# A fused attention and channel-mix kernel: the whole plan of steps put in another order

## The chip, the cores and the metric

The kernel runs on one core of a Trainium2 chip. The metric is device time in microseconds. Before the change it is 189.6 us, the median of three runs (189.48 to 189.63). Inputs and output are float32; the kernel computes in bfloat16 with sums in float32.

## The reference

Eight batches of 576 tokens, eight heads of width 64. Each head's keys and values are first pooled into 32 memories, with a softmax of `phi` over the tokens; the queries then attend to the 32 memories. The result, 512 wide, goes through a channel mix.

```
a   = softmax(phi, over tokens)                  # [b, h, 576, 32]
k_m = a^T k ;  v_m = a^T v                       # [b, h, 32, 64]
x   = softmax(q k_m^T / 8, over memories) v_m    # [b, 576, 512]
x_prev = x shifted by one token (zeros first)
xk  = mu_k * x + (1 - mu_k) * x_prev ;  xr the same with mu_r
key = relu(xk @ w_k)            # 512 -> 1024
out = sigmoid(xr @ w_r) * ((key * key) @ w_v)
```

## The kernel before

**How the work is staged.** Batch 0 goes the plain way. Its pooled k and v are made (`ekv`, L312; `kg` and `vg` are the halves for two groups of heads, `z` sums the weights in L322 and takes the reciprocal `rz` in L326), k is scaled and turned (`norm_k` and `tr_k`: `h0`, `h1`, `tk`), q is turned on VectorE (`turn_q`, L381: `q0`, `q1`), scores (`s0`, `s1`, L395) and their exponentials (`es`) follow, then the denominators (`l`: sum and logarithm, `r`: exponential of its negative, `y`: the weighing). `mixed` (L355: `mk`, `mr`) forms the token-mixed x for keys and gates; `unload` (`uk`, `ur`) copies it from PSUM to `x0T`. Sixteen keys (`c0`, L599; `a` are 256 tokens, `b` are 320) are then matmuls of `x0T` with `wk`.

Batches 1 to 7 fold the pooled v into the weights instead: v is turned (`vt`, L463, with a copy to `vT`), `project` (L492: `G`) multiplies it with `wk` and `wr`, and `keep_g` (`E`) copies the product `G` from PSUM. The keys are then *pair keys* (`c1` to `c7`, L617 and L625): two matmuls for a first part, a copy `pa` to `pb`, and four matmuls that add the difference between neighbour tokens. The softmax sums are made on VectorE by two turns and a reduction (`fe`, `fs`, `fo`: L435, L441, L447), and `w` weighs (L458). Every key is read by a relu (`r`, or the second part of `c0`) and squared (`s`). The relus keep their results in five buffers named `rl`. Gates (`g`, `t`) are matmuls followed by a tanh; outputs (`o`, L760) are eight matmuls over the squares and `wv`, multiplied by the gate on VectorE (L771) and stored.

**What sets the order.** The text table `PLAN` is the whole schedule. Each word names one step, or one part of a step, and the words are issued one after the other. Each engine takes its own instructions in that order and waits where an operand is not ready. After `/` stands the engine for copies, relus and squares (`a` ScalarE, `d` VectorE); after `@` stand the PSUM banks (numbered 0 to 7) in which the step puts its results; a bank is written only when its last reader is done. `p:` words put a load in GpSimd's queue: an f32 array in HBM, written as bf16 but for `phi`. `b:NxM` words are N filler matmuls of M times 64 columns on zeros, whose results nobody reads. Ten fillers (`WARM`) stand before the plan in both versions.

GpSimd's queue issues loads in order. In the trace before, the ninth load is issued at 10.38 us, when the first has landed, and those after it one by one as earlier ones land.

Of the kernel before, what the change touches and what calls it, by code (L numbers as in the profile page):

```python
# [19 lines left out]
    "p:q:0b 0:c01/d 0:exp1 p:v:0h 0:c00/a 0:exp0 b:11x6@5 0:mub@0 0:mub 0:kg0@12 0:c10/d 0:c11/a b:2x8@5 0:kg1",  # L20
    "0:z@0 0:q0 0:z 0:h1/a p:v:0g 0:h0/a b:7x7@5 0:tk@3 0:tk 0:q1 b:2x6@5 0:s0@1204 0:s1@3567 0:es00 0:es10",
    "0:l00@1 0:l00 b:1x4@0 0:l10@2 0:l10 0:r00 0:y00 0:r10 0:y10 0:es01 0:es11 b:9x8@0 0:l11@4 0:l01@7 0:l01",
    "0:r01 0:vg1@65 0:vg0 0:y01 0:nk0 0:l11 0:nk1 0:r11 0:y11 b:5x7@0 0:mk1@7321 0:uk11/a p:wk:4-8 0:mu@4",
    "p:wk:2-4 0:uk10/d c0:3b@0 c0:4b@2 0:tb p:wk:0-2 c0:1b@1 c0:1b/d 0:nr1 c0:3b/a c0:3b/d p:phi:1 c0:0b@7 0:nr0",
    "c0:0b/d c0:2b@0 c0:2b/d c0:4b/a 1:exp c0:1b/a c0:4b/a c0:5b@5 0:mk0@6123 0:uk00/d c0:0b/d c0:5b/a c0:2b/a",
    "c0:6b@7 0:uk01/a c0:6b/a c0:5b/d 1:z@5 0:mr0@6021 0:ur01/a 0:mu c0:7b@3 0:ur00/a c0:3a@0 c0:0a@1 c0:0a/a",
    "p:q:1 0:mr1@2674 c0:7b/d c0:7b/d 1:z c0:2a@5 c0:6b/d 0:ur10/a c0:1a@1 c0:1a/a c0:2a/a c0:5a@2 1:q1 c0:0a/a",
    "c0:6a@7 c0:7a@1 c0:2a/a c0:6a/a c0:1a/a p:k:1 1:q0 c0:3a/d 1:k@53 p:wr:0-4 1:nk/d g:01@7 1:tk@3 p:wv:2-4",
    "1:tk c0:5a/a c0:5a/a c0:3a/a c0:4a@5 p:v:1 0:ur11/a c0:7a/a c0:7a/d c0:4a/a c0:4a/d 1:s@2063 1:es1 1:es0",
    "1:fe 1:fs g:02@4 g:03@6 g:01 g:03 o:02b@0 g:00@6 x:0/a c0:6a/d g:02 1:v@23 o:03b@5 1:fo 1:nv/a 1:vt@3 1:vm",  # L30
    "g:00 1:vt/d p:phi:2 o:00b@2 o:03b 2:exp o:00b 1:G00@64 1:Gs0@37 1:G01@51 1:Es00/a 1:E001/a o:02b o:01b@2",
    "1:w0 1:w1 1:Es01/a 1:d p:wv:0-2 o:00a@0 o:00a o:01a@7 p:v:2 o:01a o:01b 1:E000/a c1:0@6 1:E010/a 1:E011/a",
    "1:Gs1@05 1:Es11/a 1:G02@14 1:E021/a 1:E020/a 1:D0 1:Gs2@73 1:Es20/d c1:0/d@5 o:02a@2 o:02a 1:Es10/a c1:2@4",
    "o:03a@7 o:03a c1:2/a@0 1:Es21/a c1:0 1:D1 c1:7@2 p:q:2 2:q0 r:100/a p:k:2 c1:7/a@3 c1:2 c1:4@6 r:120/a 2:q1",
    "c1:4/a@1 c1:7 r:170/a c1:6@4 r:171/a c1:4 r:140/d r:101/a s:10/d c1:5@2 c1:6/a@3 r:141/a s:14/a c1:5/d@5",
    "1:D2 g:11@7 r:121/a s:17/d 2:z@6 2:z c1:6 r:160/a c1:5 2:kv@10 c1:3@4 r:161/a g:11/a@3 c1:1@6 r:150/d",
    "r:151/d 2:nk/d 2:nv/d g:11 2:vt@0 c1:1/d@5 s:12/a 2:tk@1 c1:3/a@2 2:vt/d c1:3 p:phi:3 t:110 p:phi:4 2:tk",
    "t:111 r:130/a s:16/d 2:vm r:131/a c1:1 r:110/d 2:s@1437 s:13/d g:e0@0 r:111/a s:11/d 2:Gs0@65 2:es1 2:es0",
    "g:e0 s:15/d 2:fe 2:Es01/a p:k:3 2:fs 2:fo 2:G00@17 x:1/d 2:Gs1@43 2:Es00/a 3:exp 2:w0 o:13@2 g:10@6 2:Es11/a",
    "3:z@5 2:E000/a 3:z o:12@0 o:13 o:12 p:q:3 p:v:3 g:10/a@1 2:Es10/a g:10 2:E001/a 3:q1 t:100 2:D0 t:101",  # L40
    "2:Gs2@75 2:Es20/a 2:w1 2:d 2:Es21/a 2:G02@24 3:kv@63 2:G01@10 3:nk/a 2:E011/a o:e0@7 o:e0 p:q:4 c2:0@0",
    "2:E010/a 2:D1 c2:0/d@1 3:nv/a 2:E021/a 4:exp c2:2@6 o:10@3 3:q0 c2:2/a@7 o:10 3:tk@4 c2:0 2:E020/a c2:4@2",
    "c2:2 r:200/a r:201/a c2:4/a@1 3:tk r:220/d 4:q0 3:s@4035 r:221/a 3:es1 3:es0 p:v:4 c2:3@6 c2:3/d@7 s:20/d",
# [809 lines left out]
```

## Time and profile before

| | |
|---|---|
| median of three runs | 189.6 us |
| the profiled execution: first to last instruction (span) | 187.8 us |
| its own whole time | not shown; the median is 1.8 us above the span |
| TensorE (PE) busy | 181.2 us, 96% |
| VectorE (DVE) busy | 153.9 us, 82% |
| ScalarE (ACT) busy | 151.9 us, 81% |
| GpSimd (POOL) busy | 30.2 us, 16% |
| granted TensorE clock | 1.00 throughout |

A matmul counts as busy from its start to its modelled end, and these overlap; so a busy TensorE is judged by the distance between starts. VectorE and ScalarE also start an instruction before the one ahead has quite ended. "Idle before" is time in which an engine had nothing running, with what ended it. `PEld` is the load of weights, which runs beside the matmuls.

### The profile page before, as it was taken

The numbers are of one execution on the slowest core, as the hardware profiler recorded it, in microseconds if no ns is written. First come the engines' busy times: TensorE is split into PE (matmuls) and PEld (weight loads), VectorE is DVE, ScalarE is ACT, GpSimd is POOL, SyncE is SP. The second block draws the span as 40 slices with busy tenths as digits, with TensorE's granted clock in tenths as the row PEclk, the third lists the DMA queues.
The fourth block names the chain that finished last, engine by engine and source line by source line (L and its number), as shares of the span: only waits on it lengthen the run. The fifth ranks groups of instructions, "written<-read, shape, count | busy, mean of one in ns | idle before, by whom it ended". The sixth has DMA issues, their size and how long they took to land.

```text
span 187.8 us, 6010 instructions
## 1 busy us (share of the span) xinstructions
PE 181.2 (96%) x2483; PEld 103.2 (55%) x2483; DVE 153.9 (82%) x328; ACT 151.9 (81%) x368; POOL 30.2 (16%) x46
## 2 busy tenths in 40 slices
PE   7979999999999999999999999999999999999992
PEld 2544566677644575556544655556545653465441
DVE  2334574899989999999999899999989999889441
ACT  2537889889999999999999889958999678775900
POOL 5943531060303040140032000000000010000000
PEclk9999999999999999999999999999999999999999
DMA  5999999999999999899989995114202224242054
GB/s 188 280 203 220 251 207 205 266 208 234 308 208 210 275 292 255 160 220 224 223 163 237 234 278 197 28 59 113 56 0 59 58 59 113 56 108 63 0 139 140
DMA packets 24923, 31.91 MB, mean 170 GB/s; under 512 B 1880, under 2 KB 19040, under 8 KB 24896
## 3 DMA queue, kind: packets, MB, share of 16 engines
q0 software_dynamic: 17936, 20.45, 59.0%
q1 hardware_dynamic: 5664, 9.00, 17.2%
q10 hardware_dynamic: 1296, 2.08, 3.3%
q8 instruction: 19, 0.31, 0.7%
q14 instruction: 8, 0.07, 0.1%
HBM read 38.28 MB, written 9.44 MB: 254 GB/s over the span
## 4 chain that ended last, share of the span: by engine, by line
PE 90%; DMA 4%; DVE 2%; issue 1%; ACT 1%; POOL 0%; POOLq 0%; DVEq 0%
PE pv L760 34%; PE pk L617 8%; PE pk L625 8%; PE pb L625 7%; PE gps L492 6%; PE pk L599 4%; DMA q<-in_q_dram 4%; PE pr L687 3%; PE pb L687 3%; PE pr L679 3%; PE kvps L312 3%; PE pr L709 2%; PE pr L666 2%; PE scps L395 2%; PE idle L259 1%
## 5 line engine op out<-in xcount | busy, mean ns | idle before, releaser
L760 PE MATMUL pv<-wv,sq 128*128 128x512 bf16 (+3 forms) x296 | 60.5, 350 | 0.0
L760 PEld LDWEIGHTS <-sq 128*128 128x128 bf16 x296 | 27.7, 98 | 24.9 <-issue 2.8
L498 ACT CAST G<-gps 128x512 bf16<-128x512 f32 x67 | 36.2, 629 | 1.2 <-PE gps L492 1.2
L771 DVE SCALAR_TENSOR_TENSOR o<-sg,pv 128x512 f32<-128x512 f32 (+3 forms) x41 | 24.9, 613 | 7.5 <-PE pv L760 5.1
L625 PEld LDWEIGHTS <-G 128*128 128x128 bf16 x224 | 21.4, 98 | 8.5 <-issue 0.7
L583 ACT ACTIVATE rl<-pk 128x288 bf16<-128x288 f32 (+2 forms) x49 | 20.0, 420 | 4.5 <-PE pk L625 3.9
L625 PE MATMUL pk<-diff,G 128*128 128x288 bf16 x112 | 22.9, 286 | 0.0
L625 PE MATMUL pb<-diff,G 128*128 128x288 bf16 x112 | 22.9, 286 | 0.0
L617 PE MATMUL pk<-atn,G 128*128 128x288 bf16 x112 | 20.8, 287 | 0.0
L621 ACT COPY pb<-pk 128x288 f32<-128x288 f32 x41 | 16.4, 410 | 5.1 <-PE pk L617 3.5
L591 DVE TENSOR_TENSOR sq<-rl 128x576 bf16<-128x576 bf16 (+2 forms) x46 | 18.3, 420 | 1.0 <-ACT rl L583 0.5
L583 ACT ACTIVATE rl<-pb 128x288 bf16<-128x288 f32 x40 | 16.2, 427 | 2.2 <-PE pb L625 1.8
L589 ACT ACTIVATE sq<-rl 128x576 bf16<-128x576 bf16 (+2 forms) x26 | 15.7, 624 | 0.5 <-DVE rl L585 0.4
L501 DVE TENSOR_TENSOR G<-G 128x1024 bf16<-128x1024 bf16 x21 | 14.3, 679 | 1.3 <-ACT G L498 1.3
L458 DVE TENSOR_TENSOR atn<-e,lz 128x576 bf16<-128x576 bf16 (+2 forms) x18 | 12.1, 683 | 3.5 <-ACT lz L430 3.5
L617 PEld LDWEIGHTS <-G 128*128 128x128 bf16 x112 | 10.2, 98 | 6.6 <-issue 1.5
L656 ACT ACTIVATE sg<-pr 128x512 f32<-128x512 f32 x22 | 13.0, 618 | 0.7 <-PE pr L687 0.6
L259 PE MATMUL idle<-zeros 128*128 128x512 bf16 (+3 forms) x47 | 12.2, 408 | 1.0 <-DVE zeros L187 1.0
L381 DVE STREAM_TRANSPOSE qT<-q 128x576 uint32<-128x576 uint32 (+2 forms) x16 | 12.1, 765 | 1.2 <-DMA q<-in_q_dram 1.2
L585 DVE TENSOR_SCALAR rl<-pk 128x288 bf16<-128x288 f32 (+2 forms) x23 | 10.1, 449 | 2.8 <-PE pk L599 2.6
L498 DVE CAST G<-gps 128x512 bf16<-128x512 f32 x17 | 11.3, 679 | 0.2 <-PE gps L492 0.2
L292 ACT ACTIVATE em<-ph 128x1152 bf16<-128x1152 f32 (+1 forms) x9 | 9.9, 1095 | 1.6 <-DMA ph<-in_phi_dram 1.6
(101 smaller groups left out, 283.7 us busy)
## 6 DMA issues: line engine op xcount, KB each, us to landing
out_dram<-o SPq DMA_DIRECT2D x46, 128.0 KB, 2.4
ph<-in_phi_dram POOLq DMA_DIRECT2D x7, 576.0 KB, 12.2
q<-in_q_dram POOLq DMA_DIRECT2D x7, 576.0 KB, 13.6
kv<-in_k_dram POOLq DMA_DIRECT2D x7, 576.0 KB, 14.2
kv<-in_v_dram POOLq DMA_DIRECT2D x7, 576.0 KB, 15.0
out_dram<-o SPq DMA_DIRECT2D x6, 256.0 KB, 6.5
out_dram<-o SPq DMA_DIRECT2D x20, 64.0 KB, 2.5
k0f<-in_k_dram ACTq DMA_DIRECT2D x2, 576.0 KB, 5.8
```

The source lines that it names most:

```text
L259: nc.tensor.matmul(ps.rearrange("p (a b) -> p a b", b=64), lhsT=zeros, rhs=zeros[:, :64].unsqueeze(1).to_broadcast([128, blocks, 64]), sta ...
L498: return lambda: copier()(g_tile()[:, v, c, GCOLS[i]], st["gps", v, i][c])
L501: return lambda: nc.vector.tensor_sub(g_tile()[:, 1, :, GCOLS[i]], g_tile()[:, 2, :, GCOLS[i]], g_tile()[:, 0, :, GCOLS[i]])
L583: nc.scalar.activation(rl, ps, AF.Relu, scale=HALF ** 0.5)
L589: nc.scalar.activation(dst, rl, AF.Square)
L591: nc.vector.tensor_mul(dst, rl, rl)
L617: nc.tensor.matmul(pa, lhsT=st["G"][:, 2, c, f], rhs=st["at"][:, c, :NP], start=c == 0, stop=False, skip_group_check=True)
L621: copier()(pb, pa)
L625: nc.tensor.matmul(ps, lhsT=st["G"][:, v, c, f], rhs=st["d"][:, kind, c], start=False, stop=c == 1, skip_group_check=True)
L656: nc.scalar.activation(gated[name], ps, AF.Tanh, scale=0.5)
L760: nc.tensor.matmul(pv[:, cols], lhsT=squares, rhs=wv_sb[:, fi, cols], start=(fi == 0), stop=(fi == NF - 1))
L771: nc.vector.scalar_tensor_tensor(o[:, cols], in0=gated[name][:, cols], scalar=1.0, in1=pv[:, cols], op0=AL.add, op1=AL.mult)
```

## The change

All words of `PLAN` are placed anew, with other banks, other engines for some copies, and other loads first. The steps, the tables beside it and all functions stay as they are. The fillers become 25, after 37, so with the ten of `WARM` there are 35 after 47. The table is three lines shorter, so all line numbers of the code below it move by three: L326 before is L323 in the change.

The core of the diff (the opening, the step from batch 0 to batch 1, and a stretch in the middle):

```
 PLAN = [
-    "p:q:0b 0:c01/d 0:exp1 p:v:0h 0:c00/a 0:exp0 b:11x6@5 0:mub@0 0:mub 0:kg0@12 0:c10/d 0:c11/a b:2x8@5 0:kg1",
-    "0:z@0 0:q0 0:z 0:h1/a p:v:0g 0:h0/a b:7x7@5 0:tk@3 0:tk 0:q1 b:2x6@5 0:s0@1204 0:s1@3567 0:es00 0:es10",
-    "0:l00@1 0:l00 b:1x4@0 0:l10@2 0:l10 0:r00 0:y00 0:r10 0:y10 0:es01 0:es11 b:9x8@0 0:l11@4 0:l01@7 0:l01",
-    "0:r01 0:vg1@65 0:vg0 0:y01 0:nk0 0:l11 0:nk1 0:r11 0:y11 b:5x7@0 0:mk1@7321 0:uk11/a p:wk:4-8 0:mu@4",
...
-    "1:tk c0:5a/a c0:5a/a c0:3a/a c0:4a@5 p:v:1 0:ur11/a c0:7a/a c0:7a/d c0:4a/a c0:4a/d 1:s@2063 1:es1 1:es0",
-    "1:fe 1:fs g:02@4 g:03@6 g:01 g:03 o:02b@0 g:00@6 x:0/a c0:6a/d g:02 1:v@23 o:03b@5 1:fo 1:nv/a 1:vt@3 1:vm",
-    "g:00 1:vt/d p:phi:2 o:00b@2 o:03b 2:exp o:00b 1:G00@64 1:Gs0@37 1:G01@51 1:Es00/a 1:E001/a o:02b o:01b@2",
...
+    "0:exp1 0:exp0 p:q:0b b:3x8@0 0:mu@1 b:8x8@2 0:z@3 0:z 0:c00/a 0:c01/a b:3x8@4 0:kg0@76 0:c11/a 0:c10/d b:1x8@5",
+    "0:kg1 0:h0/a 0:h1/a 0:mub@5 0:tk@3 0:q0 0:tk b:3x8@0 0:s0@3076 0:es00 0:es10 0:q1 b:2x8@2 0:s1@0724 0:es01",
+    "0:es11 0:mub 0:l00@5 0:l00 0:r00 0:mu 0:y00 0:l01@3 0:l11@4 0:l10@6 0:l10 0:r10 0:l11 0:r11 0:l01 0:r01 p:v:0h",
+    "0:vg1@05 p:v:0g 0:vg0 0:nr1 0:nk0 0:y10 0:nk1 b:5x8@7 0:mk0@2674 0:uk00/a 0:nr0 0:y11 0:mr0@3501 0:ur01/a",
+    "0:ur00/a p:wk:4-8 0:uk01/d c0:6a@2 c0:5a@7 c0:6a/d c0:5a/d c0:5a/d 0:y01 c0:7a@6 c0:7a/a p:wk:0-2 c0:1a@5",
...
+    "c0:1b@0 1:tk@7 c0:5b/a c0:5b/a 0:tb 1:q0 1:q1 c0:6b/a c0:0b/a c0:3b/a 1:tk 1:s@5712 1:es0 c0:2a/d c0:1b/d",
+    "c0:1b/d c0:7b/d 1:es1 c0:7b/a p:wr:0-4 p:v:1 c0:6b/d c0:3b/d x:0/a c0:2a/a 1:fe 1:fs 1:fo g:01@3 g:01 g:03@1",
+    "g:02@7 g:03 1:v@60 g:00@2 g:02 1:nv/a 1:vt@5 1:vm p:wv:2-4 1:vt/a 1:Gs0@71 g:00 1:Es00/a 1:Gs2@46 p:wv:0-2",
...
+    "s:22/d 3:es0 3:es1 4:z r:240/d c2:3/d@6 r:241/a 3:fe s:24/d s:20/d p:q:6 3:fs 3:fo 3:w0 5:q1 5:q0 p:q:7 c2:5@2",
...
```

How it moves instructions, at four places. First VectorE in the opening, from the cast of batch 0's k to the turn of its second q half. `qT<-q_76` is the turn of the first half, `rz<-zps` the reciprocal, `kmT<-ktps` the copy of the turned k that the scores read. Before, and then in the change:

```order
L297 CAST kv_72<-k0f 128x576
L272 COPY mu_m<-mub 128x2x128
L273 TENSOR_SCALAR mu_m<-mub 128x2x128
L297 CAST kv_72<-k0f 128x576
L381 STREAM_TRANSPOSE qT<-q_76 128x4x160
L326 RECIPROCAL rz<-zps 128x2
L365 COPY kmT<-ktps 128x256
L381 STREAM_TRANSPOSE qT<-q_77 128x4x128
```

```order
L323 RECIPROCAL rz<-zps 128x2
L294 CAST kv_72<-k0f 128x576
L378 STREAM_TRANSPOSE qT<-q_76 128x4x160
L362 COPY kmT<-ktps 128x256
L378 STREAM_TRANSPOSE qT<-q_77 128x4x128
L269 COPY mu_m<-mub 128x2x128
L270 TENSOR_SCALAR mu_m<-mub 128x2x128
```

The reciprocal went ahead of the turn, and the two copies of `mu_m` behind both turns; one of the two casts went to ScalarE.

Second GpSimd's queue, from the `wk` loads on. `kv_73`, `q_75` and the first `ph` are batch 1's; `wr` and `wv` are the gate's and the output's weights. Before, and then in the change:

```order
L208 DMA wk<-in_moe_w_k_dram 128x4x512
L208 DMA wk<-in_moe_w_k_dram 128x4x256 x2
L177 DMA ph<-in_phi_dram 128x4x288
L181 DMA q_75<-in_q_dram 128x4x576
L181 DMA kv_73<-in_k_dram 128x4x576
L208 DMA wr<-in_moe_w_r_dram 128x4x512
L208 DMA wv<-in_moe_w_v_dram 128x8x256
L181 DMA kv_73<-in_v_dram 128x4x576
```

```order
L205 DMA wk<-in_moe_w_k_dram 128x4x512
L205 DMA wk<-in_moe_w_k_dram 128x4x256 x2
L174 DMA ph<-in_phi_dram 128x4x288
L178 DMA kv_73<-in_k_dram 128x4x576
L178 DMA q_75<-in_q_dram 128x4x576
L205 DMA wr<-in_moe_w_r_dram 128x4x512
L178 DMA kv_73<-in_v_dram 128x4x576
L205 DMA wv<-in_moe_w_v_dram 128x8x256 x2
```

Batch 1's k went ahead of its q, and its v ahead of the first part of `wv`; `wr` kept its place.

Third TensorE at the turn of batch 1's v (`vtps`) and what stands next to it. Before, and then in the change:

```order
L760 MATMUL pv<-wv,sq 128x256
L463 LDWEIGHTS vb
L463 MATMUL vtps<-identity,vb 128x128
L760 LDWEIGHTS sq
L760 MATMUL pv<-wv,sq 128x256
```

```order
L663 MATMUL pr<-wr,x0T 128x512
L460 LDWEIGHTS vb
L460 MATMUL vtps<-identity,vb 128x128
L489 LDWEIGHTS vT
L489 MATMUL gps<-wk,vT 32x512
```

Before, the eight matmuls of an output half followed the turn; in the change the projections that read the turned and copied `vT` follow directly.

Fourth VectorE in the middle, between the pair keys of batch 2, in the change: `eT`, `se` and `lz` are batch 3's softmax sums, `qT<-q_75` batch 5's two turns of q.

```order
L618 COPY pb<-pk 128x288
L432 STREAM_TRANSPOSE eT<-e 128x576
L588 TENSOR_TENSOR sq<-rl 128x576 x2
L438 TENSOR_REDUCE se<-eT 128x36
L439 RECIPROCAL se<-se 128x36
L444 STREAM_TRANSPOSE lz<-se 128x18x2x32
L455 TENSOR_TENSOR atn<-e,lz 128x576
L378 STREAM_TRANSPOSE qT<-q_75 128x576 x2
L588 TENSOR_TENSOR sq<-rl 128x576 x3
L345 TENSOR_SCALAR vb<-kvps,rz 128x64 x2
L588 TENSOR_TENSOR sq<-rl 128x576
L768 SCALAR_TENSOR_TENSOR o<-sg,pv 128x512
```

Before, other steps (a gate's copy, an output, relus and the turns of q elsewhere) stood among these.

113 rows, old and new, of the table PLAN are left out of this document.

## The prediction

> **What bounds the kernel now.** I read the page's totals, then TensorE's waits, then the busy time by stretches, then the opening in order of time, and last the loads.
>
> ```profile
> span 187.8 us, 6010 instructions
> PE 181.2 (96%) x2483; PEld 103.2 (55%) x2483; DVE 153.9 (82%) x328; ACT 151.9 (81%) x368; POOL 30.2 (16%) x46
> ...
> PE idle L259 <- DVE zeros L187: 1.0, 1, 1.0
> PE ktps L361 <- ACT kbd L337: 0.6, 1, 0.6
> PE pk L599 <- DVE x0T L545: 0.5, 1, 0.5
> PE mxps L355 <- DVE atn L458: 0.3, 1, 0.3
> PE scps L395 <- PE scps L395: 0.3, 1, 0.3
> PE kvps L312 <- DVE kv L297: 0.2, 1, 0.2
> ...
> 25.00:30.00 5.00, 5.00 (x149) 3.85 (x136) 2.77 (x7) 4.42 (x16) 0.85 (x3) 1.00 1.31 202
> 60.00:70.00 10.00, 10.00 (x181) 6.10 (x180) 9.96 (x21) 9.94 (x26) 2.23 (x3) 1.00 1.16 275
> ```
>
> The lines after the second are TensorE's waits, all of them, and two stretches of busy time (PE is the second number, DVE the fourth, ACT the fifth). TensorE's waits sum to 2.9 us, and the latest named one stands before the first key matmul at 19.75 us. After that it is busy in every stretch. So this kernel is an opening that waits for a chain, and then some 164 us of TensorE work end to end. An order can gain only in the opening; afterwards it can only lose, by letting TensorE wait or by making its work longer. VectorE and ScalarE at 9.96 and 9.94 of 10 show how little room the middle has.
>
> The opening, in order of time (start, duration, engine and line):
>
> ```profile
> 4.81 0.15 PEld L259 LDWEIGHTS <-zeros 128*128 128x128 bf16 x1 [0.28 <-issue]
> 5.21 1.56 PEld L259 LDWEIGHTS <-zeros 128*128 128x128 bf16 x10 [0.25 <-issue]
> ...
> 7.09 0.71 PE L268 MATMUL mub<-mu,sel 8*128 8x128 f32 x4
> ...
> 9.01 0.44 PE L312 MATMUL kvps<-kv,em 64*32 64x64 bf16 x36 [0.17 <-DVE kv L297]
> 9.39 0.38 PE L322 MATMUL zps<-ones,em 128*128 128x2 bf16 x9
> ...
> 10.12 0.84 DVE L381 STREAM_TRANSPOSE qT<-q 128x640 uint32<-128x640 uint32 x1 [1.17 <-DMA q<-in_q_dram]
> 10.89 0.13 DVE L326 RECIPROCAL rz<-zps 128x2 f32<-128x2 f32 x1
> 11.06 0.62 ACT L337 ACTIVATE kbd<-kvps,rz 128x128 bf16<-128x128 f32 x2 [2.24 <-DVE rz L326]
> 11.74 0.28 PE L361 MATMUL ktps<-identity,kbd 128*128 128x128 bf16 x2 [0.63 <-ACT kbd L337]
> 12.40 0.37 PE L395 MATMUL scps<-qT,kmT 32*32 32x160 bf16 x32
> 12.92 0.89 ACT L413 ACTIVATE e<-scps 128x160 bf16<-128x160 f32 x4 [1.24 <-PE scps L395]
> 13.03 0.35 PE L395 MATMUL scps<-qT,kmT 32*32 32x128 bf16 x32 [0.25 <-PE scps L395]
> 13.80 0.83 ACT L425 ACTIVATE lz<-zps 128x320 f32<-128x320 f32 x2
> 14.00 2.10 PE L259 MATMUL idle<-zeros 128*128 128x512 bf16 x9
> 14.53 0.82 ACT L430 ACTIVATE lz<-lz 128x320 f32<-128x320 f32 x2
> 17.22 0.36 ACT L425 ACTIVATE lz<-zps 128x256 f32<-128x256 f32 x1
> 17.61 0.42 ACT L430 ACTIVATE lz<-lz 128x256 f32<-128x256 f32 x1
> 17.68 0.60 DVE L521 SCALAR_TENSOR_TENSOR vm<-kvps,rz,mu_m 128x128 bf16<-128x128 f32 x2
> 18.67 0.47 PE L355 MATMUL mxps<-atn,vm 32*64 32x256 bf16 x28 [0.27 <-DVE atn L458]
> 19.75 3.54 PE L599 MATMUL pk<-x0T,wk 128*128 128x320 bf16 x24 [0.45 <-DVE x0T L545]
> ```
>
> The reciprocal rz had its input at 9.77 (9.39 + 0.38) but stood behind the turn of q, which waited for its load; kbd, ktps and the scores queued behind it.
>
> **The first key.** With rz ahead of the turn, the next limit is TensorE's own row of work. The ten warming matmuls end at 5.2 (the two weight loads above). Before the second half of the k sums there now stand 15 fillers at 0.22 (the nine at 14.00, rounded down for the overlap of the last), the sums of em 0.38, the turn of mu (0.22 assumed, bounds 0.1 and 0.7 by the mub row), and two kvps groups of 0.44: 5.2 + 3.3 + 0.4 + 0.2 + 0.9 = 10.0. The mub matmuls, 0.71, now come right behind. So kbd runs 10.1 to 10.7, ktps can start at 10.9 instead of 11.74, and 0.66 later (12.40 less 11.74) would come the scores; three fillers put in between push them to 11.75. That is 0.65 earlier. It is lost at once: the second scores take banks 0, 7, 2 and 4, and 0 and 7 still hold first scores. Their exponentials start 0.52 after the scores and four take 0.89, so the third is read at about 13.0, and the second scores start at 13.0, as before (13.03). What is left is gained on ScalarE, where the second exponentials are no longer split by logarithms: they end near 14.2, and four logarithms and four reciprocals (0.83 + 0.82 + twice 0.36 + 0.42) end at 17.4 instead of 18.03. The first mixes need only the first two pairs, done at 15.8. They also need v of batch 0, whose last half releases the queue at 15.08 below; two kvps groups, then four vm at 0.30 and a weighing at 0.45 on VectorE end at 16.8, not 18.6. The mixes take 0.47; ScalarE is free for their copies at 17.4; 0.6 later is the first key: **18.0**, so **-1.75**. Bounds: 17.6 if ScalarE is not in the way, 18.6 if the bank waits stack. A second mix stands ahead of it, work that before came after: **-0.45** (the row at 18.67).
>
> **TensorE's work.** The matmuls are the same, less twelve fillers of the opening. But the kinds are mixed more finely. What a change of kind costs:
>
> ```profile
> 48.81 0.41 PE L625 MATMUL pk<-diff,G 128*128 128x288 bf16 x2
> 49.05 0.41 PE L625 MATMUL pb<-diff,G 128*128 128x288 bf16 x2
> 49.39 0.80 PE L312 MATMUL kvps<-kv,em 64*32 64x128 bf16 x72
> ```
>
> Pair to pair it is 0.24, but 0.34 into the 64*32 group. Counted along the two orders there are 68 such changes before and 74 now: 6 x 0.1 = **+0.6**. Nothing hides this, since it lengthens TensorE's own stream.
>
> **New waits up to the first pair keys.** The loads:
>
> ```profile
> 13.12 0.74 POOL L208 DMA_DIRECT2D wr<-in_moe_w_r_dram  x1 [0.69 <-DMA kv<-in_v_dram]
> 15.08 0.88 POOL L208 DMA_DIRECT2D wv<-in_moe_w_v_dram  x1 [1.22 <-DMA kv<-in_v_dram]
> 17.38 0.75 POOL L181 DMA_DIRECT2D kv<-in_v_dram  x1 [1.42 <-DMA wk<-in_moe_w_k_dram]
> ...
> wr<-in_moe_w_r_dram POOLq DMA_DIRECT2D x1, 512.0 KB, 16.2
> ...
> wv<-in_moe_w_v_dram POOLq DMA_DIRECT2D x1, 512.0 KB, 17.0
> ...
> kv<-in_v_dram POOLq DMA_DIRECT2D x1, 576.0 KB, 18.1
> ```
>
> The last three rows are times from issue to landing: wr lands at 29.3, the first part of wv at 32.1, v of batch 1 at 35.5. The queue hands them over in order, so v, now one place up, takes wv's place and lands at 32.1 plus what 576 instead of 512 KB add: about 32.4. wr keeps its place and its 29.3, and that now matters: with 1.6 us in hand TensorE reaches the first gate at about 29.4, not held, with no slack left. v is wanted at 32.2: **+0.2**. The wv parts slide to 35 and 38 and are wanted near 35.6 and 39: free, but only just.
>
> The other new waits I walked by rows. The first keys of the second half (320 wide) wait for the copies of the last mix, 22.2 to 22.4: **+0.2**. Batch 1's scores stand directly behind its k transposes, with both turns of q in front of the copy on VectorE: **+0.35**. The second gate waits for the second exponentials to leave bank 1: **+0.1**. The turn of v has lost its cover:
>
> ```profile
> 37.18 0.22 PE L463 MATMUL vtps<-identity,vb 128*128 128x128 bf16 x1
> 37.23 1.04 PE L760 MATMUL pv<-wv,sq 128*128 128x256 bf16 x8
> ...
> L468 ACT COPY vT<-vtps 128x128 bf16<-128x128 bf16 x5 | 1.5, 307 | 0.2 <-DVE vM L473 0.2
> ```
>
> Eight output matmuls ran over the copy to vT; now the projections that read vT come next, and TensorE stands for the 0.31 of the copy: **+0.3**. The chain of reciprocal sums and G copies after it adds perhaps **+0.1**. All five together cost 0 if each engine runs ahead of my walk, 2.5 if each is twice as late.
>
> **The sum.** -1.75 - 0.45 + 0.6 + 1.25 = -0.35. The tail (the last 40 output matmuls, then two reads and stores) keeps its length. The profiled execution has a span of 187.8; its own total is not shown, the runs' median of 189.6 lies 1.8 above it, and I leave that 1.8 unchanged. So the span goes to 187.45 and the time to **189.2**.
>
> **Rivals.**
>
> *The gain is kept nearly whole (188.4).* My waits are then too long, mostly because ScalarE and VectorE overlap successive instructions. For it: TensorE shows no such waits now. Against it: the missing cover over vT and the fillers ahead of the scores stand in the order. Without the 1.25 it would be 188.0; with a third of it 188.4.
>
> *The loads hold everything (189.6).* The gates and batch 1's v cannot run before 29.3 and 32.4. If the stream is 0.4 late, the whole lead is gone. For it: landing times grow from 16.2 to 18.1 us down this list. Against: up to wr the same bytes go first.
>
> *VectorE's run in the middle (190.6).* Between pair keys of batch 2 the change puts five long VectorE steps in a row, with only squares, a short reciprocal and a weighing among them:
>
> ```profile
> L381 DVE STREAM_TRANSPOSE qT<-q 128x576 uint32<-128x576 uint32 x14 | 10.5, 764 | 0.0
> L447 DVE STREAM_TRANSPOSE lz<-se 128x1152 f32<-128x1152 f32 x7 | 9.6, 1375 | 0.0
> L441 DVE TENSOR_REDUCE se<-eT 128x36 f32<-128x1152 bf16 x7 | 9.4, 1347 | 0.1
> L435 DVE STREAM_TRANSPOSE eT<-e 128x576 uint32<-128x576 uint32 x7 | 5.4, 770 | 1.4 <-ACT e L409 1.4
> ```
>
> 0.77 + 1.35 + 1.38 + twice 0.76 is 5.0 us, some 7 with the small ones. Behind it queue the squares of four keys, which free the five rl buffers, and the read of the next output bank. TensorE has 14 pairs of key matmuls at 0.24 and some gate work, nearly 4.7 us, in front of that output. It decides once VectorE enters the run late: then 7 less 4.7, up to 2.3 us, stands open; the next output (eight matmuls) covers part, and I take 1.4 net, 190.6. Against: in these keys the change gives copies and relus to ScalarE.
>
> *The clock drops back.* All rows show the granted clock at full, and the fillers after 5.2 run at 0.23, while the first ten took 0.42 each. With twelve fewer fillers the opening is emptier. If it drops once, 4.2 us at half pace lose 2.1: 191.3. [...] No run here shows a drop.
>
> **Chances.** Forecast (188.9 to 189.5) 0.40; kept nearly whole 0.20; loads 0.13; VectorE's run 0.20; clock 0.03; a buffer wait that I did not find 0.04. The likeliest gives 189.2. A measurement here tells changes of over 0.2%, 0.38 us, from none, so faster means under 189.22: the whole second case and 0.25 of the forecast, **0.45**; the same 0.15 + 0.13, **0.28**; slower **0.27**. The range from 188.2 to 190.6 leaves out the far ends of three cases; the forecast's own is 188.9 to 189.5.
>
> **What would show it.** rz before the turn of q, and the second scores still at 13.0: then the bank conflict is right. The first key at 17.6 to 18.6. kvps for v of batch 1 not before 32. A gap of 0.3 behind the turn of v. After 42 no named wait of TensorE: then the middle was hidden; a wait there for VectorE between the keys of batches 2 and 3 means the third rival. I am wrong if the first key comes later than 19, or if TensorE's gaps after it sum to over 2 us.

## The result, and the profile after

The change makes the kernel slower: 193.84 us in the median (193.70 to 194.02) against 189.57 (189.48 to 189.63) beside it, a ratio of 1.023 (95% interval 1.0216 to 1.0245). I had predicted 189.2 us with a range up to 190.6. The profiled execution's span grew from 187.8 to 192.1 us. TensorE's last matmul ends 3.3 us later (187.48, before 184.22), and what follows it takes 1.04 us longer (4.64, before 3.60).

The page after, its totals, and TensorE's waits:

```profile
span 192.1 us, 6008 instructions
PE 182.2 (95%) x2471; PEld 101.9 (53%) x2471; DVE 154.4 (80%) x333; ACT 152.3 (79%) x363; POOL 30.1 (16%) x46
...
PE kvps L309 <- issue: 1.2, 2, 0.8
PE gps L489 <- ACT vT L465: 1.2, 1, 1.2
PE idle L256 <- DVE zeros L184: 1.0, 1, 1.0
PE zps L417 <- ACT e L410: 0.4, 1, 0.4
PE scps L392 <- DVE kmT L362: 0.4, 1, 0.4
...
25.00:30.00 5.00, 4.19 (x106) 3.06 (x104) 2.70 (x8) 4.29 (x9) 1.48 (x2) 1.00 1.23 207
30.00:35.00 5.00, 4.44 (x122) 2.17 (x120) 4.82 (x11) 4.05 (x12) 1.50 (x2) 1.00 1.41 199
35.00:40.00 5.00, 3.78 (x52) 2.22 (x52) 4.37 (x8) 3.83 (x11) 0.00 (x0) 1.00 1.23 266
60.00:70.00 10.00, 10.00 (x182) 5.34 (x181) 9.58 (x19) 9.04 (x24) 3.42 (x5) 1.00 1.20 224
70.00:80.00 10.00, 9.85 (x142) 5.94 (x140) 9.90 (x21) 9.78 (x28) 1.56 (x3) 1.00 1.12 314
```

In the kernel before, two of these stretches read:

```profile
30.00:35.00 5.00, 5.00 (x79) 2.82 (x67) 2.88 (x7) 4.97 (x16) 0.67 (x1) 1.00 1.23 252
35.00:40.00 5.00, 5.00 (x127) 3.43 (x125) 4.91 (x11) 3.75 (x9) 1.22 (x2) 1.00 1.32 219
```

TensorE (the second number) now stands for part of the time from 25 to 40 us, where it was busy throughout before; from 60 to 80 us it lacks only 0.15. The largest wait has no engine as its releaser (`issue`), and the second is the copy to `vT`. In order of time, the two places in which the opening lost most:

```profile
26.43 0.67 PE L309 MATMUL kvps<-kv,em 64*32 64x64 bf16 x62
27.91 0.23 PE L309 MATMUL kvps<-kv,em 64*32 64x64 bf16 x10 [0.81 <-issue]
...
35.34 1.38 DVE L444 STREAM_TRANSPOSE lz<-se 128x1152 f32<-128x1152 f32 x1
35.98 0.23 PE L460 MATMUL vtps<-identity,vb 128*128 128x128 bf16 x1
36.64 0.39 DVE L470 TENSOR_TENSOR vM<-vtps,mu 128x256 bf16<-128x256 bf16 x1
37.06 0.27 ACT L465 COPY vT<-vtps 128x128 bf16<-128x128 bf16 x1 [1.14 <-DVE vM L470]
37.38 0.41 PE L489 MATMUL gps<-wk,vT 64*32 64x512 bf16 x8 [1.17 <-ACT vT L465]
```

The first gap stands inside one group of 72 like matmuls with the same operands. The second: the copy to `vT` comes behind VectorE's `vM` in the table, waits for it, and `vM` stands behind the turn of the softmax sums.

How the lead grew and went, as the distance in time at equal real TensorE work (each matmul at its full-rate length, fillers left out), summed over the records of both traces; plus is the change ahead:

| at (us, in the change) | lead | what stands there |
|---|---|---|
| 18.5 | +1.75 | the first key is at 18.53 (before 19.75), and a second mix is done |
| 26.6 | +1.1 | keys behind mixes, two gaps of 0.3 (they end at 21.98 and 23.34) |
| 28.8 | -0.1 | the gap of 1.0 in the k sums |
| 34.9 | -0.8 | scores behind the turned k 0.45, the gate on bank 1 0.34 |
| 37.4 | -2.3 | the turn of v, 1.25 |
| 53.8 | -1.9 | |
| 75 | -2.2 | a gap of 0.3 at 70.7, in the keys of batch 2 |
| 186 | -2.75 | TensorE is never idle after 71.2 |

The last 0.5 of TensorE's 3.3 us is in the work sum itself, which counts a change of kind at the longer length.

### The profile page after: what moved, and what is told of

The parts are those of the page before. It is cut to its first block, busy times and chain, and to the rows that moved or that the text cites. A ratio compares the mean times of both kernels' runs of the same rounds, so it can differ in the third digit from the quotient of the medians.

```text
span 192.1 us, 6008 instructions
## 1 busy us (share of the span) xinstructions
PE 182.2 (95%) x2471; PEld 101.9 (53%) x2471; DVE 154.4 (80%) x333; ACT 152.3 (79%) x363; POOL 30.1 (16%) x46
## 4 chain that ended last, share of the span: by engine, by line
PE 89%; DVE 4%; ACT 3%; issue 1%; DVEq 0%
PE pv L757 33%; PE pk L614 7%; PE pk L622 7%; PE pb L622 7%; PE gps L489 6%; PE idle L256 5%; PE pk L596 4%; PE kvps L309 3%; PE pr L676 3%; PE pr L684 3%; PE pb L684 3%; PE pr L706 2%; PE scps L392 2%; PE zps L319 1%; ACT rl L580 1%
## 5 line engine op out<-in xcount | busy, mean ns | idle before, releaser
L495 ACT CAST G<-gps 128x512 bf16<-128x512 f32 x65 | 34.7, 619 | 1.1 <-PE gps L489 1.0
L618 ACT COPY pb<-pk 128x288 f32<-128x288 f32 x49 | 18.8, 395 | 4.3 <-PE pk L614 2.7
L588 DVE TENSOR_TENSOR sq<-rl 128x576 bf16<-128x576 bf16 (+2 forms) x49 | 19.5, 422 | 0.6 <-ACT rl L580 0.2
L614 PE MATMUL pk<-atn,G 128*128 128x288 bf16 x112 | 19.5, 286 | 0.1
L580 ACT ACTIVATE rl<-pb 128x288 bf16<-128x288 f32 x38 | 15.6, 422 | 0.4
L586 ACT ACTIVATE sq<-rl 128x576 bf16<-128x576 bf16 (+2 forms) x23 | 13.6, 603 | 2.9 <-DVE rl L582 2.7
L498 DVE TENSOR_TENSOR G<-G 128x1024 bf16<-128x1024 bf16 x21 | 13.8, 678 | 0.2
L495 DVE CAST G<-gps 128x512 bf16<-128x512 f32 x19 | 12.5, 682 | 1.5 <-PE gps L489 1.4
L256 PE MATMUL idle<-zeros 128*128 128x512 bf16 x35 | 11.2, 463 | 1.0 <-DVE zeros L184 1.0
```

Of the source, the lines that this page charges most:

```text
L256: nc.tensor.matmul(ps.rearrange("p (a b) -> p a b", b=64), lhsT=zeros, rhs=zeros[:, :64].unsqueeze(1).to_broadcast([128, blocks, 64]), sta ...
L495: return lambda: copier()(g_tile()[:, v, c, GCOLS[i]], st["gps", v, i][c])
L498: return lambda: nc.vector.tensor_sub(g_tile()[:, 1, :, GCOLS[i]], g_tile()[:, 2, :, GCOLS[i]], g_tile()[:, 0, :, GCOLS[i]])
L580: nc.scalar.activation(rl, ps, AF.Relu, scale=HALF ** 0.5)
L586: nc.scalar.activation(dst, rl, AF.Square)
L588: nc.vector.tensor_mul(dst, rl, rl)
```

## The experiments

All times are medians, with the executions' range in brackets; ratios are to the kernel before, with the 95% interval.

### Why TensorE stands inside a group of like matmuls

The page has a queue `q8 instruction` with 19 packets. In the trace each is 16 KB and some 0.95 us long, one for some 256 of TensorE's 4942 instructions (2471 matmuls and as many weight loads). Counted off in blocks of 256, those of the change's opening begin at 10.03, 15.82, 21.98 and 27.90 us, and the packets that come in between start at 13.52, 19.64 and 25.59. So each packet starts 3.5 to 3.8 us after its predecessor block, and the new block begins 2.3 us after the packet's start, each time with TensorE standing: 0.6, 0.3 and 1.0 us. In the kernel before, a block begins 2.7 to 4.4 us after its packet's start at the first four borders, without a gap of over 0.2 us: there the packets come in time.

Theory C: these gaps belong to a count of instructions, not to an operand. One filler of 512 columns becomes eight of 64, so seven matmuls more:

```diff
-    b:8x8@2
+    b:7x8@2 b:8x1@2
```

> The change with one filler of 512 columns replaced by eight of 64 columns at the same place in the opening (b:8x8 becomes b:7x8 and b:8x1): as many columns, seven matmuls (14 TensorE instructions) more. Theory C (TensorE's instructions arrive in blocks of 256, and in the opening the next block comes late): the gaps stay at the same count of instructions, so they move seven matmuls earlier in the program: the 0.8 us gap inside the 72 kvps matmuls of batch 1's k stands after about 55 of them instead of 62, the 0.6 us gap inside the kvps of batch 0's v after about 30 instead of 37; time 193.8 to 194.1 us. Rival (an operand, a PSUM bank or a semaphore holds these matmuls): both gaps stay at the same matmuls (62 and 37), 193.8 us.

Measured: 193.87 us (193.47 to 194.63), 1.0235 (1.0205 to 1.0265). The k sums of batch 1 in its timeline:

```profile
26.82 0.61 PE L309 MATMUL kvps<-kv,em 64*32 64x64 bf16 x55
27.72 0.26 PE L309 MATMUL kvps<-kv,em 64*32 64x64 bf16 x17 [0.30 <-issue]
```

62 and 10 have become 55 and 17: the gap moved by exactly seven matmuls. The border before it also moved, from a key into a mix (28 matmuls, then 4). At the first border nearly nothing is left to see (0.11 us inside the v sums), because TensorE came to these sums 0.6 us later than in the change, at 15.58; there my expectation of a gap after 30 matmuls was wrong. Blocks begin at 15.91, 21.80 and 27.72, again 2.3 us after their packets. No operand, bank or load holds these matmuls. Why these packets come as late as they do the traces don't show.

What are these gaps worth? First I took all 25 fillers of the table away:

> The change without the 25 fillers of its plan (the ten ahead of it stay): 50 TensorE instructions fewer in the opening. Theory C (late blocks of 256 instructions): each block holds more of the real work, the gaps at 15.2, 21.6 and 26.9 us shrink or go, and the lead over the kernel before at 29 us is about 1.3 us better than in the change: 192.3 to 192.8 us. Rival D (the opening is bound by loads and by the chain of waits, the gaps only take over slack): no change, 193.7 to 194.0 us. Rival E (fillers keep the clock up): granted clock falls between 6 and 18 us, 195 us or more.

194.78 us (194.47 to 195.25 but for one), 1.0275 (1.0253 to 1.0298): slower, and it doesn't answer the question, because the clock changed with it. The execution left out of that range is the profiled one, with a span of 231.8 us. Its granted clock, in 40 slices of 5.8 us:

```profile
PEclk9655777777777777777777777777777777777777
```

It was 0.5 from 9.4 to 23.0 us and 0.75 around that, to the end. From 6.0 us to the drop TensorE had been busy for 1.1 of 3.4 us, with no gap of over 0.93. Why the rest ran at 0.75 stays open. The other four executions have a mean granted clock of 0.963 to 0.965, where the four of the change have 0.994 or more; a mean that is 0.036 under full over 193 us makes some 14 us at half clock (an estimate from these means, since no trace shows these four). So rival E has the sign that it named. What the late blocks cost can't be read here.

Next, on the kernel with three places mended (below, 191.61 us), batch 1's k sums went two keys later, so that eight key matmuls come ahead of the border:

```diff
-    1:k@41 c0:0b/d 1:nk/d c0:2b/d c0:7b@6 c0:6b@2 c0:2a@4
+    c0:0b/d c0:2b/d c0:7b@6 c0:6b@2 1:k@41 1:nk/d c0:2a@4
```

> The three mended places (vT first, the last outputs, the late stores; together 191.6 us), and batch 1's k sums moved two keys later: 72 small matmuls stand behind eight more of 256 columns. Theory C (blocks of 256 instructions): the block that ends inside the k sums then holds eight key matmuls, 1.0 us of work, more in the same time, so the gap of 1.0 us at 26.5 us falls under 0.3 and batch 1's scores come no later: 190.6 to 191.0 us. Rival L (what follows waits for its operands: k's turn, the scores' operands, wr at 30.2): the gap goes and comes back before 31 us, 191.4 to 191.8 us.

192.16 us (190.95 to 193.11), 1.0138 (1.0107 to 1.0169), no better than without it (1.0130). The gap is gone, but:

```profile
28.07 0.75 PE L309 MATMUL kvps<-kv,em 64*32 64x64 bf16 x72
29.29 1.14 PE L596 MATMUL pk<-x0T,wk 128*128 128x256 bf16 x8 [0.47 <-DVE kbd L336]
30.27 0.28 PE L358 MATMUL ktps<-identity,kbd 128*128 128x128 bf16 x2
31.07 0.48 PE L392 MATMUL scps<-qT,kmT 32*32 32x288 bf16 x32 [0.53 <-DVE kmT L362]
```

The next key wants a bank that the scaling of k still reads, and the scores stand for the turned k. Rival L, then. I took these two waits away as well:

```diff
-    c0:2a@4 ... 1:tk@7 ... 1:s@5712 ... g:01@3 g:01
+    c0:2a@7 ... 1:tk@4 ... g:01@3 1:s@5412 ... g:01
```

> The kernel with the three mended places and the later k sums (192.2 us) with its two new waits taken away: the key behind the k sums gets bank 7 instead of bank 4 (0.55 us), and the gate g:01 goes ahead of batch 1's scores, over the wait for the turned k (0.6 us). Theory C (blocks of 256 instructions): the next block cannot start sooner than some 5.8 us after the one before, so of the 1.15 us only 0.5 to 0.7 can be had before the turn of v, with a new short gap near the v sums at the block's border; 191.2 to 191.7 us. Rival L (operands alone set the pace): all of the 1.15 us is gained up to the turn of v, 190.7 to 191.1 us.

192.76 us (191.57 to 193.73), 1.0176 (1.0143 to 1.0210). Both waits went to 0.2 or nothing, and a third of 1.15 us came, at the next gate: its bank is one that the scores' exponentials still read, and the gate that had covered them was now ahead.

```profile
31.86 0.48 PE L392 MATMUL scps<-qT,kmT 32*32 32x288 bf16 x32 [0.20 <-DVE kmT L362]
33.50 1.89 PE L663 MATMUL pr<-wr,x0T 128*128 128x512 bf16 x8 [1.15 <-ACT e L406]
```

From the first key to the turn of v it takes 17.45 us with the gap, 17.21 with the k sums moved, 17.22 with all three waits changed. So the late blocks are shown as the cause of the gaps, but at most 0.25 us of them could be had in two tries. Their own price stays open.

The medians of these two kernels are a little too high for another reason. In the profiled execution of the last one the granted clock was 0.5 from 16.5 to 19.9 us, ahead of the first key (19.81), so the 17.22 holds. Three of its six executions have a mean granted clock of 0.989 to 0.991, and two of the six before it 0.988 and 0.989. The others took 191.57 to 192.38 us and 190.95 to 192.32 us, so neither is clearly better than 191.61.

### The turn of v, and the stores

Theory A: the 1.25 us behind the turn of v are lost for good. Two words swapped:

```diff
-    1:vt@5 1:vm p:wv:2-4 1:vt/a
+    1:vt@5 1:vt/a 1:vm p:wv:2-4
```

> The change with two words swapped: the copy of the turned v (vT, on ScalarE) is issued ahead of its weighing by mu (vM, on VectorE), so that the copy no longer stands behind VectorE's turn of the softmax sums (L444, 1.38 us). Theory A (the turn of v lost its cover, and the copy queues behind VectorE): TensorE's gap behind vtps falls from 1.25 us to about 0.4, the lead over the kernel before improves by 0.8 at 37 us and this lasts to the end: 193.0 us. Rival (VectorE is what bounds this stretch; what follows waits for vM and the G copies anyway): the gap moves to the next projections, 193.6 to 193.9 us.

The gap fell to 0.43 us and batch 2's k was turned 1.13 us earlier (51.94, in the change 53.07), as theory A says; 0.31 of this was there at the first key already (18.22 and 18.53), so the swap gives 0.82. But the time was 194.1 us (193.56 to 194.63), 1.0241 (1.0219 to 1.0263): nothing gained. Rows from 65 to 70 us show where it went:

```profile
65.41 1.44 DVE L378 STREAM_TRANSPOSE qT<-q 128x576 uint32<-128x576 uint32 x2 [1.39 <-DMA q<-in_q_dram]
...
68.88 0.30 PE L392 MATMUL scps<-qT,kmT 32*32 32x288 bf16 x2 [0.72 <-DVE kmT L362]
69.47 0.48 PE L392 MATMUL scps<-qT,kmT 32*32 32x288 bf16 x30 [0.29 <-DVE o L768]
```

VectorE, now early, stands for q of batch 4, and behind it in VectorE's row is the copy of batch 3's keys that TensorE wants. That q landed at 65.39 us (in the change 64.59, in the kernel before 62.54), k of batch 3 at 61.78 (before 53.69, in another place of the queue). Up to q of batch 4 both orders load the same arrays. What differs is SP's queue, first of the change and then of the kernel before (start, length, issues), from 44 and from 38 us on:

```profile
45.64 15.97 SPq L742 DMA_DIRECT2D out_dram<-o  x10
...
61.09 1.19 SPq L745 DMA_DIRECT2D out_dram<-o  x2
```

Five outputs of batches 0 and 1 are held in SBUF and stored by `w:` words. The change has three of these (768 KB) at 45 to 57 us, while loads follow each other (42.55, 45.41 and 48.24 us are the landings of three of 576 KB, 2.85 us apart). The kernel before stores nothing until 61 us. I had not looked at the `w:` words at all. Theory F: the early stores hold up the loads. The five words moved back to where the kernel before has them, alone:

```diff
-    o:03a w:03 r:101/d
+    o:03a r:101/d
...
-    o:23 4:w1
+    o:23 w:03 w:00 4:w1
```

> The change with one edit alone: the five stores of held outputs moved back to the kernel before's places; vT, the tail and all else stay as in the change. Theory F (the loads' pace at 55 to 70 us and TensorE's lag behind the turn of v hide each other): q of batch 4 lands some 2 us earlier, but TensorE comes to batch 3's scores 1.1 us late from the turn of v anyway, so only its small waits of 67 to 71 us can go: 193.3 to 193.7 us. Rival K (the early stores alone are the loss, the turn of v costs nothing): 192.0 to 192.5 us.

193.99 us (193.02 to 194.46), 1.0222 (1.0199 to 1.0246): far from rival K, and in the median a little above what F expected. But three of the five executions have a mean granted clock of 0.987 to 0.991; the other two took 193.02 and 193.34 us, so up to 0.8 us may be gained. The profiled one (193.34) puts little of this on the loads: its first key came 0.42 us earlier than in the change, its last matmul 0.40 earlier, and its tail is 0.28 shorter. Then with the swap of `vT` and with the tail mended (below):

> The change with the swap of vT and vM, the kernel before's order of the last outputs, and the stores of the five held outputs (the words w:) moved back to where the kernel before has them, behind batch 3's and batch 4's keys. Theory F (between 55 and 70 us the loads set the pace: the early stores take bandwidth from them, k of batch 3 and q of batch 4 land at 61.8 and 65.4 us, VectorE stands 1.4 us for that q and TensorE behind it): q of batch 4 lands at 63 us or earlier, TensorE's waits at 61 to 70 us fall from 1.8 us to under 0.6, the 1.1 us gained behind the turn of v are kept, and with the 0.5 of the tail the time is 192.0 to 192.5 us. Rival G (VectorE's own queue of work is the limit at 65 to 70 us, whatever the loads do): the wait for VectorE stays, 193.2 to 193.4 us.

191.61 us (191.18 to 192.46), 1.0130 (1.0106 to 1.0153). Here k of batch 3 landed at 59.44 and q of batch 4 at 62.32 us, and VectorE no longer stood for it:

```profile
63.73 0.16 DVE L506 TENSOR_SCALAR diff<-atn 128x2 bf16<-128x2 bf16 x1
63.79 1.43 DVE L378 STREAM_TRANSPOSE qT<-q 128x576 uint32<-128x576 uint32 x2
```

It beat F's range by 0.4 us. The three edits together give 2.2 us. The two traces divide the 2.4 between their spans: 0.46 at the first key (18.07 and 18.53), which no edit explains, 0.82 from the swap, and 1.13 in the tail (3.51 and 4.64), more than the tail's order alone gave. The swap's 0.82 is kept only with late stores: from batch 2's turned k to the last matmul it takes 134.4 us in the change, with late stores alone and with all three, but 135.6 with the swap alone, which met the loads. So late stores shorten this stretch only if TensorE comes to it early, and coming early helps only with late stores. The swap and the stores were not run together without the tail.

If only VectorE's place for these turns were at fault, moving them later should do as well (stores left early, swap and tail mended):

```diff
-    4:q0 4:q1 2:D1 ... 3:es0 3:es1 4:z
+    2:D1 ... 3:es0 3:es1 4:q0 4:q1 4:z
```

> The change with the swap of vT and vM and the kernel before's order of the last outputs, and batch 4's two turns of q moved behind the exponentials of batch 3; the stores stay early. Theory F: VectorE no longer stands for the late q of batch 4 ahead of the copy of batch 3's keys, so TensorE's wait for the scores of batch 3 (0.8 and 0.6 us) goes, the wait for k of batch 3 (0.3) stays: 192.3 to 192.8 us. Rival G (VectorE's own work is the limit): the wait only moves behind the later turns, 193.2 to 193.4 us.

193.90 us (193.72 to 195.87), 1.0255 (1.0221 to 1.0289): worse than F and than G. k of batch 3 still held TensorE, and behind the moved turns the relus came late:

```profile
PE pk L614 <- DVE rl L582: 1.5, 1, 1.5
...
PE kvps L309 <- DMA kv<-in_k_dram: 0.4, 1, 0.4
```

Are early stores a loss in any order? Into the kernel before, three of them at the change's places:

```diff
-    o:03a@7 o:03a c1:2/a@0 ... 2:nk/d 2:nv/d g:11
+    o:03a@7 o:03a w:03 c1:2/a@0 ... 2:nk/d 2:nv/d g:11 w:02 w:00
```

> The kernel before with three stores moved early, to where the change has them (o:03 behind its second half at some 48 us, o:02 and o:00 behind batch 2's scaled v at some 52 us); all else as before. Theory F (early stores cost nothing by themselves; they delay the loads, and that counts only where the order takes the loads just as they land): k of batch 3 and q of batch 4 land 1 to 2 us later, but the kernel before uses them 4 and 5 us after they land, so 189.4 to 189.8 us. Rival K (the early stores are a loss in any order): 190.5 us or more.

190.22 us (190.00 to 190.69), 1.0048 (1.0036 to 1.0061): a loss of 0.5%, where I expected none. The mechanism is F's, the place is one that I had not checked. k and q had 4 us to spare, but v of batch 3 had not: it landed at 61.28 instead of 59.66, and its sums, which ran at 60.73 without a wait, now stand:

```profile
61.42 0.80 PE L312 MATMUL kvps<-kv,em 64*32 64x128 bf16 x72 [0.76 <-DMA kv<-in_v_dram]
```

### The tail

In the change, `o:73` is read ahead of `o:70`, whose matmuls are done first; so the first read waits, and four stores come to SP at once. The kernel before's order in its place:

```diff
-    o:70@3 o:73@1 o:73 x:7/a o:e3@7 o:70 o:e3
+    o:70@3 o:70 o:73@1 x:7/a o:e3@7 o:73 o:e3
```

> The change with the last outputs read in the kernel before's order: o:70 is read at once and o:73 and o:e3 one after the other, instead of o:73 and o:70 together behind o:73's matmuls. Theory B (stores bunch up in SP's queue at the end): span's end minus TensorE's end falls from 4.6 us to 3.6, 192.8 us. Rival (the end is set by the last read and the last store's landing alone): at most 0.3 us, 193.5 to 193.8 us.

193.34 us (193.13 to 193.37), 1.0197 (1.0179 to 1.0215): 0.5 us, between theory B and its rival. First the change, then this kernel, VectorE's first reads and SP's stores at the end:

```profile
182.38 1.28 DVE L768 SCALAR_TENSOR_TENSOR o<-sg,pv 128x512 f32<-128x512 f32 x2 [5.44 <-issue]
183.10 5.75 SPq L742 DMA_DIRECT2D out_dram<-o  x10
```

```profile
180.70 0.69 DVE L768 SCALAR_TENSOR_TENSOR o<-sg,pv 128x512 f32<-128x512 f32 x1 [3.71 <-ACT rest L647]
181.41 6.86 SPq L742 DMA_DIRECT2D out_dram<-o  x10
```

The ten issues begin 1.7 us earlier though TensorE ends at the same time (187.5). From there to the span's end it takes 3.9 us, not 4.6.

### The two halves

The change's order up to the turn of batch 1's v (with `vT` first), then what remains in the kernel before's order:

> The change's order up to the turn of batch 1's v (with the copy to vT first), then the steps that remain in the kernel before's order, with its banks, its stores and its tail. This puts the opening apart from the rest. If the losses are as the trace of the change reads (opening 0.5 to 0.8 us behind by then; the middle, the drift and the tail the rest), 190.0 to 190.6 us. Rival H (the opening leaves loads and buffers so late that the middle loses as well, whichever order follows): 191.5 us or more. Rival I (the opening's lag is made up in the middle, where the kernel before has slack): 189.3 to 189.7 us.

191.14 us (189.98 to 191.38), 1.0071 (1.0045 to 1.0096). The lowest two executions (189.98 and 190.12) are at the lower end of the forecast range, the other three over half a microsecond above it. In the profiled one, the slowest of the five, the k turns of batches 2 to 5 all come 0.98 to 1.01 us after those of the kernel before, so the opening costs 1.0 there; another 0.9 goes at 104 us:

```profile
103.55 0.43 PE L392 MATMUL scps<-qT,kmT 32*32 32x288 bf16 x19
104.60 0.34 PE L392 MATMUL scps<-qT,kmT 32*32 32x288 bf16 x13 [0.62 <-issue]
```

That is a block's border again. The packet started at 102.07, 2.5 us before the matmuls go on; in the kernel before, at the same place in the program, at 95.58. Why it came late here I can't say.

With the k sums two keys later in this graft:

> The change's opening with vT first and batch 1's k sums two keys later, then the kernel before's order. Against the same without the moved k sums (191.1 us in the median, 190.0 in the lowest executions). Theory C: 0.9 us less, 189.1 to 190.2 us. Rival L: 190.0 to 191.2 us.

191.20 us (190.32 to 192.29), 1.0084 (1.0057 to 1.0112): no gain, as rival L has it, nor among the four executions whose mean granted clock is 0.996 or more (190.32 to 191.38).

The opposite half, the kernel before up to batch 1's first projections and then the change's order with its places mended:

> The opposite half: the kernel before's order up to the first projections of batch 1, then the change's order with the late stores and the kernel before's order of the last outputs. It gives what the change's order costs behind the opening. If the three mended places and the opening are all of it, 189.4 to 189.8 us. If the finer mixing of the kinds of matmul costs what the prediction took for it (6 more changes of 0.1 us) and no more, 189.9 to 190.3 us. If the middle holds a further loss, 190.6 us or more.

197.90 us (197.31 to 198.12), 1.0435 (1.0416 to 1.0454). This says nothing on the change's middle. The seam itself loses some 5 us, since projections and outputs meet there with the copies of `G` still to do, and then the clock drops; the longest row, and the granted clock in 40 slices of 4.9 us:

```profile
43.09 1.87 PE L760 MATMUL pv<-wv,sq 128*128 128x256 bf16 x8 [2.17 <-ACT G L498]
...
PEclk9999999975999999999999999999999999999999
```

The granted clock was 0.5 from 41.8 to 48.7 us, so these eight matmuls took 1.87 instead of 1.04 us. All four executions have a mean of 0.980 to 0.988. TensorE was busy for 5.6 us of that stretch, so, as an estimate from that, the clock takes up to 2.8 of the loss at the seam and the waits the rest.

From batch 2's turned k on it takes 134.41 us, as in the change. What the change's order costs there against the kernel before was not measured apart.

### The first term alone

The kernel before with the reciprocal ahead of the turn of q, and nothing else:

```diff
-    0:z@0 0:q0 0:z
+    0:z@0 0:z 0:q0
```

> The kernel before with one word moved: batch 0's reciprocal (the second 0:z) ahead of the first turn of q, nothing else. The prediction's first term alone: kbd and the turned k 0.6 us earlier, here without a bank conflict of the scores; first key 0.3 to 0.6 us earlier than 19.75 us, 189.0 to 189.3 us. Rival C (blocks of instructions pace TensorE between 16 and 36 us): the first key is earlier but the lead is gone by 36 us, 189.5 us. Rival J (the first key waits for ScalarE's logarithms or for v, not for the reciprocal): first key at 19.7 us, 189.5 us.

189.55 us (188.85 to 190.03), 1.0004 (0.9992 to 1.0017). The first key comes 0.56 us earlier, at 19.19. The sums of batch 1's em, `zps`, at 24.11 take all but 0.1 of it:

```profile
21.85 1.16 ACT L292 ACTIVATE em<-ph 128x1152 bf16<-128x1152 f32 x1 [0.34 <-DMA ph<-in_phi_dram]
...
24.11 0.36 PE L322 MATMUL zps<-ones,em 128*128 128x2 bf16 x9 [0.37 <-ACT rl L583]
```

ScalarE, early now, stands for the phi of batch 1, which lands at 21.83; a relu queued behind it frees the bank late. That is neither C nor J: an engine that takes its steps in order waits for a load, and the lead ends there. Two tries to open the way:

```diff
-    1:exp c0:1b/a c0:4b/a ... 1:z@5
+    c0:1b/a c0:4b/a 1:exp ... 1:z@4
```

> The kernel before with the reciprocal ahead of the turn of q, and besides it the exponential of batch 1's phi two squares later on ScalarE and batch 1's sums of em in bank 4 instead of 5. Theory M (behind the first key the loads hold the opening: ScalarE stood 0.3 us for phi with relus queued behind, then wr lands at 29.9 and v of batch 1 at 35.4 us, just where they are used): the lead of 0.5 us now passes 24 us, and ends at the first gate, which waits for wr at 29.9 us; 189.3 to 189.6 us. Rival N (only phi and bank 5 were in the way): the lead stays to the end, 189.0 to 189.2 us.

189.77 us (189.27 to 190.32), 1.0020 (1.0008 to 1.0032). The first key came at 18.76, the first gate at 29.88 (before 30.08). But bank 4, which I had chosen, holds the turned mu until 24.07, so `zps` stood for that. Then both moved behind the gate mixes:

> The kernel before with the reciprocal ahead of the turn of q, and batch 1's exponential of phi and its sums of em both moved behind the gate mixes (the exponential behind the copies of the first gate mix, the sums behind the second), so that neither phi nor a bank holds the first mixes and keys. Theory M (the loads stop the lead next): TensorE is 0.5 us or more ahead of the kernel before at 25 us, reaches the first gate at 29.8 to 29.9 us, when wr has landed, and the v sums at 35.3 us, when v has: 189.2 to 189.6 us. Rival N (only phi and the bank were in the way): the first gate at 29.3 us or earlier and the lead stays to the end, 188.8 to 189.1 us.

189.96 us (189.46 to 190.62), 1.0031 (1.0018 to 1.0045). The mixes ran 1.2 us earlier (23.29, before 24.51), and then:

```profile
26.38 0.38 PE L322 MATMUL zps<-ones,em 128*128 128x2 bf16 x9 [0.41 <-ACT em L292]
27.02 2.34 PE L599 MATMUL pk<-x0T,wk 128*128 128x256 bf16 x20 [0.26 <-DVE rz L326]
```

Three orders, three other waits, one result: the first gate at 29.9 to 30.0 and no gain. The v sums ran at 35.65, with v landed at 35.60, so 0.15 us of waiting for that load is seen. Whether `wr`, in at 29.6 to 29.9, would have been next can't be told: TensorE never got there early enough.

## Why the prediction was wrong, step by step

**The first key: right.** 18.53 against 18.0 with bounds of 17.6 and 18.6, and +1.75 of lead with the second mix, against 2.2. The bank conflict is as told: second scores at 13.12 (13.0). ScalarE's logarithms ended at 17.69 (17.4). How near the number came is partly luck: in eight traces that have the same opening up to there at full clock the first key comes at 17.89 to 19.02 us.

**TensorE's work: right in kind.** By the records there are 78 changes of kind now and 70 before; at the 0.095 us of one such change that is 0.76, against 0.6. Without the fillers it is 72 and 66, six more as I had counted.

**The new waits: the step that failed.** I had 1.25 us (at most 2.5) behind the first key, and measured about 3.6. By parts: v of batch 1, 0.2 expected, nothing seen (landed at 33.0, used at 34.26); the 320-wide keys 0.2, measured 0.3; scores behind the turned k 0.35, measured 0.45; the gate on bank 1 0.1, measured 0.34; the turn of v 0.3, measured 1.25; and 1.3 of gaps at the borders of instruction blocks, which no step had. At the turn of v I took the length of the copy for the wait, without asking what the copy itself waits for: VectorE's row at that point.

**"The middle was hidden": true of this execution, but not for the reason I had.** Of my signs, "after 42 no named wait of TensorE" came true but for 0.15 us, and I would have taken it for a proof. But the middle hid a limit that no rival named: with stores moved into the stretch of loads, batch 3's k and batch 4's q land just as the late TensorE wants them. The rival on loads ended at 33 us, and the rival on VectorE's run cost 0.3 at 70.7; neither looked at SP's queue. In this execution the stores cost TensorE nothing that shows (134.4 us from batch 2's turned k on, early stores or late), since the lateness from the opening was there already. They cost the chance to make up 0.8 of it.

**"The tail keeps its length": wrong by 1.04 us.** I counted its matmuls and not the order of its reads. Of this, 0.5 came back in the time with one pair of words swapped (the tail by the traces: 4.64, then 3.91); with late stores as well the tail is 3.51, shorter than before the change.

**The clock: right.** No execution of the change has a mean granted clock under 0.994. But the 0.03 that I had given a drop was an estimate with no trace of a drop to go by, and the margin was small. In two traces with this opening (the changed banks, and the first graft with later k sums) the clock fell to 0.5 at 16.5 us, for 3.4 us where I had taken 4.2; in the 3.4 us ahead of it TensorE was busy for 2.3 to 2.4 and no gap was over 0.52. In the change's own trace, at a granted clock of 1.00, TensorE was busy for 2.5 of the same stretch, not much more.

**The 1.8 us around the span: right,** 1.74 now.

**What is left.** With the three places mended the kernel is at 191.61, still 2.2 us over the kernel before (189.38 beside it). The first graft's trace, one of its slower executions, puts 1.0 of this in the opening. From 53.8 us to the last matmul the change loses 1.35 (0.85 of lead and the 0.5 in the work sum), while TensorE is idle for 0.15 in all. Seven of the eight added changes of kind lie there, which by the count is 0.67; mixing was not tested alone, and the remainder has no cause that the record shows. No version tried beats the kernel before.

## What to carry to other kernels

In this order, tuned as a whole, a gain at the front was worth only what the next in-order queue let through: of the 0.56 us that the reciprocal alone gave, 0.1 was left behind the load of phi. So follow a gain to the next load, bank and engine row before counting it, and look at every queue past which something moved, the stores' too. A wait's length is not that of the last instruction ahead of it, but what that instruction stands behind: 1.25 us at the turn of v, where the copy itself took 0.27. And two edits that give little alone can gain together where one delay hides the other (the swap of `vT` kept its 0.82 us only with late stores), so undoing one part at a time can miss both. Last, look at the granted clock of every execution before comparing medians: here it explains a part of several that read like waits.

## What the hardware showed that I had not expected

In both traces 19 packets of 16 KB stand in the instruction queue, one for some 256 of TensorE's instructions. In the change's opening the packet for the next block started 3.5 to 3.8 us after the current block began (counted in the same way, some 1 to 3.5 us in the middle, and between 2.5 us ahead of it and 1.2 behind from 119 us on), and the block could begin 2.3 us after the packet. So this opening of many small matmuls, two instructions each, passed no more than 256 instructions in 5.3 to 6.2 us, there and with seven matmuls more.

The granted clock fell to 0.5 though TensorE never stood for a whole microsecond in the 3.4 us ahead: busy for 1.1 with no gap over 0.93 (no fillers), and busy for 2.3 to 2.4 with no gap over 0.52 (the two kernels named above). What decides on a drop is not shown.

768 KB of stores among back-to-back loads delayed a later load by 1.6 us in the kernel before (v of batch 3).
